# Stores into GpSimd's queue, and the loads of one batch taken apart around the transposes (Linformer attention and an MLP-mixer, one core)

## The chip, the core and the metric

The kernel runs on one core of one Trainium2 chip. The metric is the device time of one execution in microseconds; the number that counts is the median of several executions. In the text TensorE is PE, VectorE is DVE, ScalarE is ACT, GpSimd is POOL and SyncE is SP, as in the profile. "SPq" is SP's instruction queue, which only issues transfers here.

## What is computed

The inputs are q, k, v of shape (8, 8, 1024, 64): batch, heads, sequence, head size. E and F have shape (64, 1024), and there are four weight matrices. With biases and checks left out, the reference is

```python
k_proj = np.einsum('ks,bhsd->bhkd', E, k)
v_proj = np.einsum('ks,bhsd->bhkd', F, v)
scores = np.matmul(q, k_proj.transpose(0, 1, 3, 2)) / np.sqrt(64)
attn = softmax(scores)                      # over the 64 projected keys
x = np.matmul(attn, v_proj)                 # heads side by side: (8, 1024, 512)
h = np.maximum(x.transpose(0, 2, 1) @ w_tok1, 0.0) @ w_tok2   # 1024 -> 256 -> 1024
u = x + h.transpose(0, 2, 1)
h2 = np.maximum(u @ w_ch1, 0.0) @ w_ch2     # 512 -> 1536 -> 512
return (u + h2).astype(np.float32)
```

## The kernel before

The work of a batch b falls into two parts.

**The front** of a batch makes u. `kv_proj` projects k and v of all eight heads (lines 455 and 458) with copies to `kp` and `vb` by DVE and ACT; `k_transpose` (L492) turns the projected keys, and DVE and ACT copy them to `kT` (L502, L507); `scores` is one matmul per head (L555) and an exponential on ACT (L564); `attend` is four matmuls per head (L578), with a reciprocal and a multiplication on DVE (L590, L595) into `x_sb`; `token1` (L609) and `token2` (L629) are the token MLP, and DVE adds x to it (L640) into `u`. `scores` needs `qT`, which is q transposed: on PE for batches 0 and 1, and by two DMA transposes of SP (`q_transpose`, L519) for batches 2 to 7. When four of the eight row tiles of `u` are there, a DMA transpose of SP (L649) writes half of `uT`, so that each batch has a u transpose 0 and a u transpose 1, which the text calls u(b, 0) and u(b, 1).

**The back** is the channel MLP. Sub-block j = 2b + i works on half i of batch b. It begins with the sums of quarters of `uT` on DVE (`s_sums`, L671), four additions or subtractions that stand together; then `up_set` runs three sets of seven products (L801), and `down_block` seven products (L896) in the order 1, 7, 6, 2, 5, 3, 4, each product being two times six matmuls. Between products 5 and 3 of a `down_block` DVE must read a bank (`da`, L943). ACT copies other banks to `o` and `db` (L925), POOL adds u in place (L927), DVE writes the rest (L947, L955), and each sub-block stores two output tiles of 512 KB (`store`, L920). There are three output buffers, and one `db`.

Every instruction is a job of a planner (`Planner.plan`), which orders the jobs by its own estimate of times and by due times (`prio`). The jobs of PE, DVE, ACT and POOL are issued in the planned order, and each engine's queue is kept in it. Transfers are jobs on a model engine "DMA" and are put into the program where the planner's list has them; from there they stand in the queue of the engine that issues them, in order with what else this engine does. Loads of q, k and v convert from float32 to bfloat16 and are issued by POOL (L314), in pieces of four heads from batch 1 on. In the kernel before, stores and transposes are issued by SP.

`tie(j, other)` makes transfer j wait for transfer other to land. `load_batch(b)` (L979) issues all six loads of batch b after the attention of batch b - 1, tied to the transpose that was planned last (`turned[0]`); a u transpose is tied to the last load that was planned (`landed[0]`). The place where the front of a batch lies between the sub-blocks is given by due times: `front(b, at - 62, at - 14)`, where `at` is the due time of the first sub-block of batch b.

Of the kernel before, what the change touches and what calls it, by code (L numbers as in the profile page):

```python
# [34 lines left out]
class Planner:  # L35
# [4 lines left out]
    def __init__(self, caps, homes):  # L40
        self.jobs, self.caps, self.homes = [], caps, homes
        self.wrote, self.readers = {}, {}

    def add(self, eng, occ, lat, fn, reads=(), writes=(), prio=None, takes=(), uses=(), after=()):
        j = Job(len(self.jobs), eng, occ, lat, fn, prio)
# [26 lines left out]
    def plan(self):  # L72
        for j in self.jobs:
            for d in j.deps:
                d.next.append(j)
        for j in reversed(self.jobs):
            if j.prio is None:
                due = [s.prio for s in j.next]
                j.prio = (min(due) if due else 1e9) - j.occ - 0.3
        for j in self.jobs:  # L80
            if j.prio > 1e8:
                j.prio = max((d.prio for d in j.deps), default=0) + 2
        free = {}
        waiting = {j.n: len(j.deps) for j in self.jobs}
        can = {}
        est = {}

        def open_(j):
            est[j.n] = max((d.end + self.LAG[d.eng] if d.eng != j.eng else d.full for d in j.deps), default=0.0)
            can.setdefault(j.eng, []).append(j)  # L90

        for j in self.jobs:
            if not waiting[j.n]:
                open_(j)
        bank_free = [0.0] * 8
        clean = [True] * 8
        held = dict.fromkeys(self.caps, 0)
        left = {}
        for j in self.jobs:
            for b in j.banks:  # L100
                left[id(b)] = left.get(id(b), 0) + 1
        order = []
        turn = {n: [b for j in self.jobs for b in j.takes if b.stream == n] for n in self.caps}

        def home(b, now):

            if held[b.stream] == self.caps[b.stream]:
                return None
            if b.stream in "UD" and turn[b.stream][0] is not b:
                return None  # L110
            best = None
            keep = [i for i in self.homes["U"] if clean[i] and bank_free[i] is not None]
            if all(clean[:5]):
                keep = []
            for i in self.homes[b.stream]:
                t = bank_free[i]
                if t is None or (b.seeded and not clean[i]):
                    continue
                if not b.seeded and clean[i] and keep and keep[-1] == keep[0] == i:
                    continue  # L120
                c = (max(now, t), clean[i], t, i)
                if best is None or c < best:
                    best = c
            return best

        while any(can.values()):
            pick = None
            for e, js in can.items():
                f = free.get(e, 0.0)
                cands = []  # L130
                for j in js:
                    t = max(f, est[j.n])
                    spot = None
                    if j.takes:
                        h = home(j.takes[0], t)
                        if h is None:
                            continue
                        t, spot = h[0], h[3]
                    cands.append((t, j.prio, j.n, j, spot))
                if not cands:  # L140
                    continue
                t0 = min(c[0] for c in cands) + 0.02
                c = min((c for c in cands if c[0] <= t0), key=lambda c: (c[1], c[2]))
                if pick is None or c[0] < pick[0]:
                    pick = c
            if pick is None:
                raise RuntimeError("no job can go on", [(j.eng, j.fn.__qualname__, j.prio) for js in can.values() for j in js][:20], held, bank_free)
            t, _, _, j, spot = pick
            can[j.eng].remove(j)
            j.start, j.end, j.full = t, t + j.lat, t + j.lat + 0.03  # L150
            free[j.eng] = t + j.occ
            if j.takes:
                b = j.takes[0]
                b.at = spot
                turn[b.stream].remove(b)
                held[b.stream] += 1
                bank_free[spot] = None
            for b in j.banks:
                left[id(b)] -= 1
                if not left[id(b)]:  # L160
                    held[b.stream] -= 1
                    bank_free[b.at] = max(x.end for x in b.jobs) + 0.1
                    clean[b.at] = b.full
            order.append(j)
            for s in j.next:
                waiting[s.n] -= 1
                if not waiting[s.n]:
                    open_(s)
        assert len(order) == len(self.jobs), (len(order), len(self.jobs))
        return order  # L170


@with_exitstack
def kernel(
# [333 lines left out]
            writes=[("kT", 1, h) for h in heads], uses=[bk],  # L508
        )

    turned = [None]
    landed = [None]

    def q_transpose(due):
        for h in range(0, H, H // 2):
            before = turned[0]
            turned[0] = sp(
                3.5,
                lambda h=h: nc.sync.dma_start_transpose(  # L519
                    out=qT[:, h : h + H // 2].rearrange("p h j s -> p (h j) s"),  # L520
                    in_=q_sb[:, h : h + H // 2].rearrange("p h si d -> p (h si d)"),
                ),
                reads=[("q", i) for i in range(h, h + H // 2)],
                writes=[("qT", i) for i in range(h, h + H // 2)], prio=due,
            )
            if before:
                turned[0].deps.add(before)

    def q_transpose_pe(hp, due):
        bk = Bank(stream[0], full=False)  # L530
# [93 lines left out]
    def token2(b, si, due):  # L624
        bk = Bank(stream[0], full=False)

        def mm():
            for t in range(TC):
                nc.tensor.matmul(  # L629
                    bank(bk), wt2_sb[:, t, si::NSI], hT_sb[:, t, :],  # L630
                    start=(t == 0), stop=(t == TC - 1),
                )

        pe(
            TC, 512, mm, reads=["wt2"] + [("hT", t, hp) for t in range(TC) for hp in range(HP)],
            takes=[bk], prio=due,
        )
        dve(
            512,
            lambda: nc.vector.tensor_add(  # L640
                out=u_t[b % 2][:, si, :], in0=bank(bk), in1=x_sb[:, si, :]
            ),
            reads=[("x", h, si // NJ) for h in range(H)], writes=[("u", b % 2, si)], uses=[bk],
        )
        if si % NJ == NJ - 1:
            i = si // NJ
            j = sp(
                3.5,
                lambda: nc.sync.dma_start_transpose(  # L649
                    out=uT_t[i].rearrange("p s dc q -> p (s dc) q"),  # L650
                    in_=u_t[b % 2][:, i * NJ : (i + 1) * NJ].rearrange("p s d -> p (s d)"),
                ),
                reads=[("u", b % 2, n) for n in range(i * NJ, (i + 1) * NJ)],
                writes=[("uT", i, n) for n in range(HP)], prio=None,
            )
            if landed[0]:
                tie(j, landed[0])
            turned[0] = j

    def quarter(j, sh, dh):  # L660
        return uT_t[j % 2][:, 2 * sh : 2 * sh + 2, 2 * dh : 2 * dh + 2, :]
# [209 lines left out]
    def down_block(j):  # L871
# [30 lines left out]
        def product(n, i):  # L902
# [5 lines left out]
            for t in range(2):  # L908
# [5 lines left out]
                    prio=due_d(j, 2 * i + t),  # L914
                )

        def store(sh):
            rows = slice(i * NJ + 2 * sh, i * NJ + 2 * sh + 2)
            sp(
                1.5, lambda: nc.sync.dma_start(out=out_v[b, :, rows, :], in_=o_t[os[sh]]),  # L920
                reads=[o_key(sh, 0), o_key(sh, 1)], prio=None,
            )

# [52 lines left out]
            u_transpose_pe(hp, i, (-5.5 if i == 0 else 1.5) + 0.5 * hp)  # L976
    stream[0] = "F"

    def load_batch(b):  # L979
        jobs = [load_heads(b, n, hh, H // 2, None) for n in "kvq" for hh in range(0, H, H // 2)]  # L980
        for j in jobs if turned[0] else ():
            tie(j, turned[0])
        landed[0] = jobs[-1]

    def front(b, begin, end):
        units = []
# [5 lines left out]
        for i in range(H // hn):  # L992
            unit(1.9 * hn / H, lambda t, i=i: kv_proj(b, i * hn, hn, t))
            unit(0.9 * hn / H, lambda t, i=i: k_transpose(i * hn, hn, t))
            if b == 1:
                for hp in range(2 * i, 2 * i + 2):
                    unit(0.4, lambda t, hp=hp: q_transpose_pe(hp, t))
        unit(0.4, lambda t: scores(0, t))
        unit(0.4, lambda t: scores(1, t))
        for h in range(H):  # L1000
            if h + 2 < H:
                unit(0.4, lambda t, h=h: scores(h + 2, t))
            for half in range(2):
                unit(0.25, lambda t, h=h, half=half: attend(h, half, t))
        if b + 1 < B:
            unit(0.0, lambda t: load_batch(b + 1))
        for n in range(TC):
            unit(1.8, lambda t, n=n: token1(n, t))
        for si in range(NSI):
# [10 lines left out]
    for b in range(B):  # L1020
# [5 lines left out]
        if b + 1 < B:  # L1026
            at = 2 * TU * (b + 1)
            if b > 0:
                q_transpose(None)
            front(b + 1, at - 62, at - 14)  # L1030
    gate = mybir.DependencyInfo(mybir.DependencyClass.Sync, mybir.DependencyReason.DATA)
    plan = pl.plan()
# [41 lines left out]
```

The softmax here doesn't subtract the row's maximum and nothing guards it: scores larger than these inputs give would overflow.

## Time and profile before

| | |
|---|---|
| time, median of 8 runs (lowest to highest) | 440.41 us (438.84 to 440.97) |
| time of the profiled execution, and its span | 439.02 us, 437.0 us |
| mean granted clock of TensorE | 0.988 |
| busy: PE, DVE, ACT, POOL | 415.9, 320.9, 241.2, 106.3 us |
| POOL's DMA queue | 29.36 MB, 42.6% of the 16 DMA engines' span |
| SP's and ACT's DMA queue (stores, transposes) | 30.68 MB, 28.9% |
| median time to landing: store, k, v, q load | 3.6, 8.8, 12.8, 11.3 us |
| median time to landing: u transpose, q transpose | 4.6, 5.2 us |

The span is the time from the first to the last recorded instruction; about 2 us of the execution's time lie around it. Busy time of PE comes from a model of pipelined matmuls: a matmul of 256 columns is shown with 0.27 us, and in a row of them one starts every 0.109 us. The time to landing is counted from the issue and so includes time in the queue.

### The profile page before, as it was taken

What the parts mean: (1) busy time and instruction counts of PE and PEld (TensorE: products, weight loads), DVE (VectorE), ACT (ScalarE), POOL (GpSimd) and SP (SyncE); (2) the same over time, 40 slices, a digit from 0 to 9 for tenths busy, and PEclk for the clock granted to TensorE, in tenths of its full rate; (3) what the DMA queues carried; (4) which work ended last, traced back from release to release, by engine and by line L of the source; (5) the groups of instructions that cost most, each with busy time, mean ns of one, the idle gap of its engine ahead of it and who ended that gap; (6) DMA issues with size and microseconds to landing.
All of it is one profiled execution on the core that took longest, in us unless ns stands there. A gap on an engine that the chain in (4) does not pass through costs nothing.

```text
span 437.0 us, 9315 instructions
## 1 busy us (share of the span) xinstructions
PE 415.9 (95%) x3736; PEld 336.7 (77%) x3736; DVE 320.9 (73%) x783; ACT 241.2 (55%) x439; POOL 106.3 (24%) x122
## 2 busy tenths in 40 slices
PE   6689999999999999999999999999999999999993
PEld 3477878678778886788778877788768886888883
DVE  3459969679888797779697696778687596966451
ACT  1658785258545755557355654657446663555540
POOL 8542131032301332115021331115011210212212
PEclk9799999999999999999999999999999999999998
DMA  9999999198946899198955699096983711251022
GB/s 167 208 199 206 207 149 209 64 199 169 174 82 167 124 196 172 52 206 154 199 88 124 136 199 215 3 207 132 206 133 68 175 48 56 43 145 68 29 98 96
DMA packets 89515, 60.89 MB, mean 139 GB/s; under 512 B 55680, under 2 KB 84864, under 8 KB 89472
## 3 DMA queue, kind: packets, MB, share of 16 engines
q0 software_dynamic: 30624, 29.36, 42.6%
q1 hardware_dynamic: 58768, 30.68, 28.9%
q8 instruction: 29, 0.48, 0.4%
q10 hardware_dynamic: 80, 0.26, 0.3%
q14 instruction: 14, 0.11, 0.1%
HBM read 59.24 MB, written 16.78 MB: 174 GB/s over the span
## 4 chain that ended last, share of the span: by engine, by line
PE 86%; DVE 8%; ACT 3%; DMA 1%; issue 1%; DVEq 0%; ACTq 0%
PE ps L896 32%; PE ps L801 30%; PE ps L609 6%; PE ps L629 5%; PE ps L555 3%; PE ps L578 3%; PE ps L455 3%; DMA uT<-u 1%; DVE S L671 1%; DVE u L728 1%; ACT qT L547 1%; PE ps L377 1%; PE ps L539 1%; PE ps L689 1%; DVE da L943 1%
## 5 line engine op out<-in xcount | busy, mean ns | idle before, releaser
L896 PEld LDWEIGHTS <-G 128*128 128x128 bf16 x1344 | 130.1, 98 | 24.3 <-issue 5.5
L896 PE MATMUL ps<-wc_sb,G 128*128 128x256 bf16 x768 | 103.8, 273 | 3.7 <-DVE da L943 2.6
L801 PEld LDWEIGHTS <-wc_sb 128*128 128x128 bf16 x768 | 73.6, 98 | 14.3 <-issue 1.6
L823 ACT ACTIVATE G<-ps 128x512 bf16<-128x512 f32 x96 | 57.2, 599 | 39.8 <-PE ps L801 39.6
L896 PE MATMUL ps<-wT,G 128*128 128x256 bf16 x576 | 77.7, 273 | 0.0
L927 POOL TENSOR_TENSOR o<-o,u 128x512 f32<-128x512 f32 x32 | 37.6, 1175 | 129.2 <-ACT o L925 114.0
L801 PEld LDWEIGHTS <-wT 128*128 128x128 bf16 x576 | 55.1, 98 | 11.2 <-issue 2.2
L801 PE MATMUL ps<-uT,wc_sb 128*128 128x256 bf16 x384 | 57.6, 273 | 0.0
L801 PE MATMUL ps<-S,wc_sb 128*128 128x256 bf16 x384 | 57.6, 273 | 0.0
L927 POOL TENSOR_TENSOR db<-db,u 128x512 f32<-128x512 f32 x16 | 18.8, 1175 | 157.5 <-ACT db L925 157.5
L801 PE MATMUL ps<-S,wT 128*128 128x256 bf16 x384 | 54.9, 273 | 0.9 <-ACT G L823 0.7
L640 DVE TENSOR_TENSOR u<-ps,x_sb 128x512 bf16<-128x512 f32 x56 | 35.7, 684 | 22.2 <-PE ps L629 21.7
L595 DVE TENSOR_TENSOR x_sb<-ps,rdn 128x256 bf16<-128x256 f32 x128 | 49.7, 415 | 0.3
L836 DVE TENSOR_TENSOR G<-G 128x512 bf16<-128x512 bf16 x96 | 46.7, 489 | 3.4
L782 DVE CUSTOM_DVE_ANT_0 g<-ps,ub 128x512 bf16<-128x512 f32 x48 | 32.8, 684 | 20.5 <-PE ps L801 20.4
L782 DVE CUSTOM_DVE_ANT_0 G<-ps,ua 128x512 bf16<-128x512 f32 x48 | 32.8, 682 | 18.1 <-ACT ua L829 17.9
L564 ACT ACTIVATE a<-ps 128x512 bf16<-128x512 f32 x64 | 37.1, 600 | 12.2 <-PE ps L555 12.0
L829 ACT COPY ua<-ps 128x512 f32<-128x512 f32 x48 | 28.2, 587 | 24.2 <-PE ps L801 23.6
L829 ACT COPY ub<-ps 128x512 f32<-128x512 f32 x48 | 28.2, 587 | 9.6 <-PE ps L801 9.1
L842 ACT COPY ps<-ps 128x512 f32<-128x512 f32 x48 | 28.2, 588 | 6.9 <-DVE g L782 4.2
L578 PE MATMUL ps<-vb,a 128*128 128x130 bf16 x256 | 30.4, 223 | 0.6 <-DVE x_sb L595 0.6
L629 PE MATMUL ps<-hT_sb,wt_sb 128*128 128x512 bf16 x112 | 29.5, 379 | 0.0
(69 smaller groups left out, 516.0 us busy)
## 6 DMA issues: line engine op xcount, KB each, us to landing
out_dram<-o SPq DMA_DIRECT2D x32, 512.0 KB, 3.6
k_sb<-in_k_dram POOLq DMA_DIRECT2D x14, 512.0 KB, 8.8
v_sb<-in_v_dram POOLq DMA_DIRECT2D x14, 512.0 KB, 12.8
q_sb<-in_q_dram POOLq DMA_DIRECT2D x14, 512.0 KB, 11.3
wc_sb<-in_moe_w_ch_dram POOLq DMA_DIRECT2D x6, 256.0 KB, 12.6
wc_sb<-in_moe_w_ch_dram POOLq DMA_DIRECT2D x4, 384.0 KB, 12.2
k_sb<-in_k_dram POOLq DMA_DIRECT2D x4, 256.0 KB, 6.8
v_sb<-in_v_dram POOLq DMA_DIRECT2D x4, 256.0 KB, 7.3
```

The lines of the kernel that those rows point to most:

```text
L564: lambda: nc.scalar.activation(out=a_t[h % 4], in_=bank(bk), func=ACT.Exp, scale=scale),
L578: nc.tensor.matmul(view()[:, 2 * jj : 2 * jj + 2].rearrange("p c d -> p (c d)"), a_t[h % 4][:, j * P : (j + 1) * P], vb[:, h].rearrange("k ...
L595: lambda: nc.vector.tensor_tensor(out=x_sb[:, 4 * half : 4 * half + 4, h * D : (h + 1) * D], in0=view()[:, :, 0:D], in1=rdn[:, :, None].to ...
L629: nc.tensor.matmul(bank(bk), wt2_sb[:, t, si::NSI], hT_sb[:, t, :], start=(t == 0), stop=(t == TC - 1),)
L640: lambda: nc.vector.tensor_add(out=u_t[b % 2][:, si, :], in0=bank(bk), in1=x_sb[:, si, :]),
L782: nc.vector._custom_dve(TENSOR_ADD_SAT, out=out, in0=in0, in1=in1, s0=FMAX, s1=0.0)
L801: nc.tensor.matmul(t[:, c, :], w1_of(n, dd, 2 * m + c), a_of(j, n, dd), start=(n in (1, 7) and c == 0 and dd == 0), stop=(c == 1 and dd == 1),
L823: lambda: nc.scalar.activation(out=G[:, n, cs], in_=view(src), func=ACT.Relu),
L829: 512, lambda: nc.scalar.copy(out=dst, in_=view("y")), writes=[(name, s % 2)],
L836: 512, lambda: f(out=G[:, n, cs], in0=in0, in1=in1), ps=False, reads=deps,
L896: nc.tensor.matmul(view(X_OF[n])[:, t, :], G[:, G_OF[n], cc, t * P : (t + 1) * P], w2_of(n, cc), start=(n in (1, 7) and t == 0 and cc == 0 ...
L927: 512, lambda: nc.gpsimd.tensor_add(out=dst, in0=dst, in1=u_of(sh, dh)),
```

## The change

The stores of all sub-blocks but the last are issued by POOL, in the queue of the loads. `load_batch` is replaced. The k and v loads of batch b + 1 are planned right behind the projections of batch b, tied behind u(b - 1, 0); u(b - 1, 1) is tied behind the last of them. The q loads of batch b + 1 are planned behind the q transposes of batch b, which have finished with the buffer, and u(b - 1, 0) is tied behind the last of these. The planner lists a transfer by the time at which its inputs are ready, no longer by the time at which the model engine "DMA" would start it.

```diff
@@ Planner.plan
-                due = [s.prio for s in j.next]
+                due = [s.prio for s in j.next if s.prio is not None]
...
+        for g in self.groups:
+            first = min(j.prio for j in g)
+            for n, j in enumerate(g):
+                j.prio = first + 0.01 * n
...
+            j.at = est[j.n] if j.eng == "DMA" else t
...
-        return order
+        return sorted(order, key=lambda j: j.at)
@@ q_transpose
-    turned = [None]
-    landed = [None]
-
-    def q_transpose(due):
+    turned_u = {}
+
+    def q_transpose(b, behind):
         for h in range(0, H, H // 2):
-            before = turned[0]
-            turned[0] = sp(
+            j = sp(
...
-            if before:
-                turned[0].deps.add(before)
+            if behind:
+                j.deps.add(behind)
+            behind = j
+        if b + 1 < B:
+            last = load_group(b + 1, "q", j)
+            if b > 2:
+                tie(turned_u[b - 1, 0], last)
@@ token2
-            if landed[0]:
-                tie(j, landed[0])
-            turned[0] = j
+            turned_u[b, i] = j
@@ down_block
+        queue = nc.gpsimd if j < NSB - 1 else nc.sync
...
-                1.5, lambda: nc.sync.dma_start(out=out_v[b, :, rows, :], in_=o_t[os[sh]]),
+                1.5, lambda: queue.dma_start(out=out_v[b, :, rows, :], in_=o_t[os[sh]]),
@@ loads
-    def load_batch(b):
-        jobs = [load_heads(b, n, hh, H // 2, None) for n in "kvq" for hh in range(0, H, H // 2)]
-        for j in jobs if turned[0] else ():
-            tie(j, turned[0])
-        landed[0] = jobs[-1]
+    def load_group(b, names, behind):
+        jobs = [load_heads(b, n, hh, H // 2, None) for n in names for hh in range(0, H, H // 2)]
+        for j in jobs if behind else ():
+            tie(j, behind)
+        return jobs[-1]
+
+    def load_kv(b):
+        last = load_group(b, "kv", turned_u.get((b - 2, 0)))
+        if (b - 2, 1) in turned_u:
+            tie(turned_u[b - 2, 1], last)
@@ front
+        if b + 1 < B:
+            unit(0.0, lambda t: load_kv(b + 1))
+        if b == 1:
+            unit(0.0, lambda t: load_group(2, "q", None))
         unit(0.4, lambda t: scores(0, t))
...
-        if b + 1 < B:
-            unit(0.0, lambda t: load_batch(b + 1))
@@ the loop over batches
             if b > 0:
-                q_transpose(None)
+                q_transpose(b + 1, turned_u.get((b - 1, 1)))
             front(b + 1, at - 62, at - 14)
```

More of the change, by code (lines that the diff above doesn't have):

```diff
@@ L42, in __init__ @@
         self.wrote, self.readers = {}, {}
+        self.groups = []
     def add(self, eng, occ, lat, fn, reads=(), writes=(), prio=None, takes=(), uses=(), after=()):
@@ L523, in q_transpose @@
                 reads=[("q", i) for i in range(h, h + H // 2)],
-                writes=[("qT", i) for i in range(h, h + H // 2)], prio=due,
+                writes=[("qT", i) for i in range(h, h + H // 2)], prio=None,
             )
-            if before:
-                turned[0].deps.add(before)
+            if behind:
[5 more added lines that the diff above has]
+                tie(turned_u[b - 1, 0], last)
     def q_transpose_pe(hp, due):
```

## The prediction

> **What bounds the kernel now.** I read the busy times first. PE is busy in 95% of the span:
>
> ```profile
> PE 415.9 (95%) x3736; PEld 336.7 (77%) x3736; DVE 320.9 (73%) x783; ACT 241.2 (55%) x439; POOL 106.3 (24%) x122
> ```
>
> The windows of 25 us show where the rest is (the first columns are length and PE's busy time):
>
> ```profile
> 100.00:125.00 25.00, 25.00 (x209) 19.20 (x209) 22.40 (x62) 14.73 (x28) 6.81 (x8) 1.00 0.96 171
> 275.00:300.00 25.00, 24.54 (x229) 20.97 (x224) 19.38 (x40) 15.35 (x29) 5.09 (x5) 1.00 0.50 107
> 350.00:375.00 25.00, 24.45 (x201) 18.92 (x200) 20.11 (x56) 12.14 (x22) 2.31 (x2) 1.00 0.22 64
> ```
>
> PE is full from 100 to 275 us, and loses about half a microsecond in each later window. The rest is at the start (waiting for inputs) and in the last 12 us, whose order the change leaves alone. The timeline of PE names the stalls (in brackets: idle time, and who ended it):
>
> ```profile
> 91.20 0.81 PE L896 MATMUL ps<-wc_sb,G 128*128 128x256 bf16 x6 [0.85 <-DVE da L943]
> 280.61 0.82 PE L896 MATMUL ps<-wc_sb,G 128*128 128x256 bf16 x6 [0.46 <-DVE da L943]
> 325.45 0.60 PE L801 MATMUL ps<-S,wT 128*128 128x256 bf16 x4 [0.73 <-ACT G L823]
> 355.88 0.27 PE L578 MATMUL ps<-vb,a 128*128 128x130 bf16 x2 [0.55 <-DVE x_sb L595]
> 379.23 0.81 PE L896 MATMUL ps<-wc_sb,G 128*128 128x256 bf16 x6 [0.44 <-DVE da L943]
> ```
>
> Idle time starts where the modelled 0.27 us of a matmul ends, while the next could start after 0.109; so each costs 0.16 more: 3.03 + 5 x 0.16 = 3.8 us. Adding all steps (0.109 a matmul of 256 columns, 0.216 of 512, 0.057 in `attend`, 1.85 for the projections of eight heads) from matmul 790 at 88.2 us to the last gives 8.0 us less than the trace: these 3.8, 2.2 in the tail, and 2.0 in pieces of 0.25 or less. So this change, which takes no matmul away, can win 5.8 us at most.
>
> Transfers reach PE only through others. The chain of waits shows it once:
>
> ```profile
> 267.68 6.25 DMA uT<-u
> 273.95 0.43 DVE S L671
> 274.98 1.65 DVE S L671 x3
> 279.96 0.61 DVE da L943
> 280.61 0.82 PE ps L896 x6
> ```
>
> A u transpose takes 6.25 us here because loads and a store are in flight; alone it takes 4.3. DVE waits for it in its queue, and `da` and PE behind DVE.
>
> **The parts.** I compared the instruction order of both programs. PE's order is the same up to matmul 790, and the tail's. In between, scores come much earlier behind the projections: 2.0 to 2.6 us of PE work after `k_transpose` instead of 10 to 18. Token matmuls come in fours and twos between the products instead of 16 in a row. I place events of the changed program at 88.2 us plus the steps of its order.
>
> *Stores to POOL.* 30 stores leave SP. SP's waits for POOL in front of stores add up to 187.7 us, but the transposes behind them were not late for that alone: u(b, 1) must also wait for the previous odd sub-block to have read `uT1`. POOL gets 30 issues; the rows of its load issues say 0.70 to 0.87 us, so 30 x 0.77 = 23 us on an engine that is busy for 106 of 437. Behind a store POOL waits for the last DVE instruction of a sub-block; next in its queue is the `db` addition of the next sub-block, some 10 us later. An output buffer is used again 16 us or more after its store is issued, and a store lands in 2.6 to 8.8 us, or some 10 us more behind four loads. Cost: nothing; if that cover were gone, DVE's L955 would hold a bank. The Trainium skill speaks against this part: SBUF — State Buffer, "SBUF: two separate sides", says that a transfer issued by GpSimd cannot get its descriptors written while VectorE holds the shared port, and advises the queue of ScalarE or SyncE instead; it gives 3.1 us instead of 0.62 for a small transfer. By that the stores would land later, and the sum would not change, since nobody waits for them; in this trace 66 issues by POOL beside a DVE that is busy for 73% stay between 0.56 and 0.87 us.
>
> *Stalls removed.* The stall at 91.2: the new order has three scores (0.65) between product 5 and product 3 of that sub-block, so 0.65 goes. At 280.6 and 379.2 DVE came late to `da` behind the four sums S. In the new order no load is tied to run beside u(5, 0) and u(7, 0), the sums stand at 269 and 368, and the next `da` at 298 and 372: 0.62 + 0.60 go. At 325.5 ACT stood behind `kp` copies, at 355.9 DVE behind a subtraction that took 1.38 us beside a POOL addition (0.41 normally); these can come back elsewhere, so half of 0.89 + 0.72. Of the 2.0 in small pieces I take 0.5. Sum: -3.2, between -0.65 and -4.5.
>
> *Scores close behind kT.* From the last matmul of L492 to the end of ACT's copy L507 the six full-width cases took 1.99, 2.33, 2.02, 2.00, 2.59, 2.21 us. The new order leaves 1.8 us for batch 2, 2.0 for batch 3 and 2.4 for the others. Stalls with 0.1 for the semaphore: 0.3 + 0.4 + four times nothing or 0.3. I take +0.8, between 0 and 2.4 (the 2.59 for all).
>
> *The ties.* u(b, 0) waits for the two q loads of batch b + 2. Example b = 4: the q transposes follow u(3, 1) and last 9 us for two (289.02 to 297.84 in POOL's wait), so to 202; a first load lands 5.3 us after its issue (147.48 to 152.78), the next 2.55 later: 210. u(4, 0) is complete at 215. No wait; for b = 3 the q load sits behind a POOL addition and lands at 168, 2.4 us after u, but DVE has nothing to do for PE until 176. Cost: 0.
>
> u(b, 1) waits for four k and v loads, which wait for u(b, 0), for the projections of batch b + 1 and, in POOL's queue, for an addition in front. For b = 3, 4, 5 the issue comes at 175.7, 225.2 and 274.3 (projections end at 174.6, 223.9, 273.2; the addition takes 1.2). Landing of the fourth: 5.3 + 3 x 2.55 = 13.0 later, and then the transpose, 4.3 alone. But the two stores of the sub-block now sit right behind these loads in the same queue and move at the same time as the transpose, so I take the 6.25 of the row above (6.7 is the longest). Ready at 195.0, 244.5, 293.6. PE needs the sums only at 207, 256, 306, but DVE's queue has them behind reciprocals of 193.2, 242.6 and 291.9, with 0.8 of multiplications: it arrives at 194.0, 243.4, 292.7 and waits 1.0 + 1.1 + 0.9 = 3.0 us in the midst of the attention. Queued behind are reciprocals and `add_relu`, and behind those PE, which has three banks for the front and other products to run. DVE is idle for a quarter of the time and can catch up. Nothing to all of it reaches PE; I take a third, +0.9, nearest to the single case at 273.95, where 0.64 of waiting and a slow sum cost 0.62. For b = 1 (ready 110, needed by DVE at 110.9) and b = 2 (147, 150) I count 0.
>
> Sum: -3.2 + 0.8 + 0.9 = -1.5. The profiled execution took 439.02 (span 437.0 and 2 around it), so 437.5; it lies 1.39 under the median of 440.41. Taken from the median: 438.9.
>
> **Rivals.** *The stalls only move*: PE waits at kT and at the sums as much as it did at `da`. For it: both new margins are under half a microsecond. Against: the front is spread more evenly, which DVE's 22.4 us in the window from 100 to 125 shows to be needed. Price: -3.2 + 2.4 + 0.9 = +0.1, that is 440.5.
>
> *The tie blocks DVE* (slower): u(b, 1) lands later than I think, since the loads take longer. In the trace a group of loads with two stores beside it needed 16.9 us from its first issue to the fourth landing (152.87 to 169.73) where I count 13.0. With 3.9 us more, DVE waits about 4.9 us in each of three batches; at half of it on PE this is 7.4 instead of 0.9, so 440.41 + 5 = 445.4. It decides from the point where DVE waits 2.2 us in each of the three: half of 6.6 is 3.3, which with the 0.8 at kT makes up for the 3.2 and passes no change by 0.9 us. Against: with stores behind the loads and transposes kept apart, the group runs alone.
>
> *The change does not do what it says*: the tie could be dropped where two transfers share a predecessor. The order shows it in place: u(4, 1) waits for the last v load of its group.
>
> **Numbers.** The forecast has 0.55 (436.4 to 439.5), no change 0.2 (439.5 to 441.3), the blocked DVE 0.25 (441.3 to 445.4). A difference of 0.2%, 0.88 us, is about what a measurement can tell; these cases are cut there, so the chances of faster, same and slower are the same three. The range goes from 436.4, where the stalls go and almost nothing comes, to 442.8, which leaves about 0.15 out above and 0.05 below.
>
> **What would show it.** Right: no `da` stall at the first sums of a batch, no store in SP's waits, q and k/v loads in two groups per batch, DVE waiting for `uT` about 1 us near 194, 244 and 293. Wrong: DVE waiting over 2 us there, PE waiting for kT in each batch over 0.5, or POOL late with `db`.

## The result, and the profile after

The changed kernel took 443.96 us (median of 12 runs, 441.21 to 446.48), the kernel before 439.06 (33 runs, 438.78 to 442.22) in the same comparison: a ratio of 1.010, with a 95% interval of 1.0081 to 1.0119. In another comparison it was 443.37 to 440.16, or 1.0084 (1.0054 to 1.0114). The change makes the kernel slower by about 1%, 3 to 5 us, where 1.5 us less were forecast. The profiled execution took 442.56 us, with a span of 440.6.

PE's work is the same, and its busy time differs little. The busy times and the shares of the chain of waits, from the page of the kernel after:

```profile
PE 418.0 (95%) x3736; PEld 336.7 (76%) x3736; DVE 321.0 (73%) x783; ACT 242.9 (55%) x439; POOL 122.9 (28%) x152
...
PE 75%; DVE 12%; DMA 8%; ACT 2%; issue 1%; DVEq 0%; ACTq 0%
PE ps L904 26%; PE ps L809 26%; DMA uT<-u 8%; PE ps L639 5%; PE ps L619 5%; PE ps L462 3%; PE ps L588 3%; PE ps L565 3%; DVE S L679 2%; DVE x_sb L605 2%; DVE G L844 2%; DVE g L790 1%; DVE u L736 1%; PE ps L549 1%; PE ps L384 1%
```

8% of the chain that ended last, some 35 us, is now u transposes (`uT<-u`). In the kernel before all transfers together had 1%, and DVE waited for a u transpose once:

```profile
PE 86%; DVE 8%; ACT 3%; DMA 1%; issue 1%; DVEq 0%; ACTq 0%
...
DVE S L671 <- DMA uT<-u: 0.6, 1, 0.6
```

The waits of the kernel after (total, times, longest) name who stands there:

```profile
SPq L659 <- DMA v_sb<-in_v_dram: 96.7, 5, 21.6
...
DVE S L679 <- DMA uT<-u: 7.6, 6, 2.3
...
PE ps L809 <- DMA uT<-u: 2.4, 1, 2.4
...
PE ps L588 <- DVE x_sb L605: 1.7, 3, 0.9
```

The first line is the tie at work: SP holds five u(b, 1) until the last v load has landed. The second is DVE standing at the first sum of a sub-block; before, this was one wait of 0.64 us. The third is PE itself waiting for a transpose; before, this did not occur. In the fourth PE waits for the attention's multiplication, which in two of the three cases (near 251 and 302) is queued behind the sums on DVE. One such place can be read in the chain of the kernel after (start, duration, what):

```profile
244.30 6.34 DMA uT<-u
250.64 0.02 issue
250.66 0.42 DVE S L679
251.09 0.34 DVE x_sb L605
251.42 0.33 DVE S L679
...
252.07 0.43 DVE x_sb L605
252.50 0.04 issue
252.55 0.27 PE ps L588 x2
```

u(4, 1) lands at 250.64, DVE (idle, as its timeline says, for 1.55 us) has been waiting for it since 249.1, and behind the sums stand the multiplications whose banks PE needs. The timeline of PE shows the two largest stalls ahead of the tail, whose own are as before (in brackets: idle time and who ended it):

```profile
114.92 0.61 PE L809 MATMUL ps<-uT,wc_sb 128*128 128x256 bf16 x4 [2.43 <-DMA uT<-u]
...
251.48 0.27 PE L588 MATMUL ps<-vb,a 128*128 128x130 bf16 x2 [0.85 <-DVE x_sb L605]
```

The windows of 25 us at the three places shown before (length, then PE's busy time) put this in place:

```profile
100.00:125.00 25.00, 22.57 (x185) 17.55 (x183) 19.31 (x51) 12.30 (x23) 1.67 (x3) 1.00 0.99 178
275.00:300.00 25.00, 25.00 (x234) 20.41 (x232) 19.92 (x51) 17.07 (x32) 7.65 (x9) 1.00 0.81 150
350.00:375.00 25.00, 24.93 (x206) 19.81 (x204) 17.87 (x44) 11.99 (x22) 4.57 (x5) 1.00 0.20 61
```

The two later windows did become full, as forecast. The first one, which had been full, lost 2.4 us.

**A measure for what follows.** PE's order is the same in both programs up to matmul 790, and yet its start lay anywhere from 88.05 to 91.5 us in the profiled executions, with kernels of either order. In the one before and the two after, it came at 88.2, 89.2 and 91.4, and the granted clock was 0.66, 0.56 and 0.51 from 10 to 20 us, and 1.00, 0.93 and 0.64 from 20 to 30. That is not the whole reason: in the profiles of E2 and E4 below the clock was 1.00 in both stretches, and matmul 790 came at 89.7. So I compare from the start of matmul 790 to that of the last one: 342.86 us before, 345.52 after, and 347.48 in a second profile of the changed kernel (E12 below). This is the part in which PE's order differs: +2.7 and +4.6. It leaves out the first 88 us, in which the change moves some transfers but no matmul.

### The profile page after: what moved, and what is told of

Its sections match the earlier page's. It is cut to its first block, busy times and chain, and to the rows that moved or that the text cites. A ratio compares the mean times of both kernels' runs of the same rounds, so it can differ in the third digit from the quotient of the medians.

```text
span 440.6 us, 9330 instructions
## 1 busy us (share of the span) xinstructions
PE 418.0 (95%) x3736; PEld 336.7 (76%) x3736; DVE 321.0 (73%) x783; ACT 242.9 (55%) x439; POOL 122.9 (28%) x152
## 4 chain that ended last, share of the span: by engine, by line
PE 75%; DVE 12%; DMA 8%; ACT 2%; issue 1%; DVEq 0%; ACTq 0%
PE ps L904 26%; PE ps L809 26%; DMA uT<-u 8%; PE ps L639 5%; PE ps L619 5%; PE ps L462 3%; PE ps L588 3%; PE ps L565 3%; DVE S L679 2%; DVE x_sb L605 2%; DVE G L844 2%; DVE g L790 1%; DVE u L736 1%; PE ps L549 1%; PE ps L384 1%
## 5 line engine op out<-in xcount | busy, mean ns | idle before, releaser
L605 DVE TENSOR_TENSOR x_sb<-ps,rdn 128x256 bf16<-128x256 f32 x128 | 50.8, 416 | 0.7
L650 DVE TENSOR_TENSOR u<-ps,x_sb 128x512 bf16<-128x512 f32 x56 | 38.0, 687 | 10.9 <-PE ps L639 9.4
L844 DVE TENSOR_TENSOR G<-G 128x512 bf16<-128x512 bf16 x96 | 43.5, 458 | 3.3
L790 DVE CUSTOM_DVE_ANT_0 G<-ps,ua 128x512 bf16<-128x512 f32 x48 | 32.9, 685 | 13.3 <-ACT ua L837 12.7
L588 PE MATMUL ps<-vb,a 128*128 128x130 bf16 x256 | 31.8, 226 | 2.0 <-DVE x_sb L605 1.7
L639 PE MATMUL ps<-hT_sb,wt_sb 128*128 128x512 bf16 x112 | 32.5, 379 | 0.0
## 6 DMA issues: line engine op xcount, KB each, us to landing
wc_sb<-in_moe_w_ch_dram POOLq DMA_DIRECT2D x4, 384.0 KB, 12.1
```

Source lines behind the costliest of these rows:

```text
L588: nc.tensor.matmul(view()[:, 2 * jj : 2 * jj + 2].rearrange("p c d -> p (c d)"), a_t[h % 4][:, j * P : (j + 1) * P], vb[:, h].rearrange("k ...
L605: lambda: nc.vector.tensor_tensor(out=x_sb[:, 4 * half : 4 * half + 4, h * D : (h + 1) * D], in0=view()[:, :, 0:D], in1=rdn[:, :, None].to ...
L639: nc.tensor.matmul(bank(bk), wt2_sb[:, t, si::NSI], hT_sb[:, t, :], start=(t == 0), stop=(t == TC - 1),)
L650: lambda: nc.vector.tensor_add(out=u_t[b % 2][:, si, :], in0=bank(bk), in1=x_sb[:, si, :]),
L790: nc.vector._custom_dve(TENSOR_ADD_SAT, out=out, in0=in0, in1=in1, s0=FMAX, s1=0.0)
L844: 512, lambda: f(out=G[:, n, cs], in0=in0, in1=in1), ps=False, reads=deps,
```

## The experiments

All runs were compared with the kernel before on the same chip; E1 to E8 ran on one chip, E9 to E12 on another. Theory A: the ties make u(b, 1) late. Theory B: the stores, in a queue of their own beside the transposes, make u(b, 1) late. Theory C: the new order of PE's work costs the time, whatever the transfers do. After eight runs three more were stated: P (what costs time is how late the transposes are against the place that the planner gave the sums), and its rivals Q (later sums are better in any arrangement) and R (the new order that a longer estimate brings makes the difference, whatever the waits).

**E1: no u transpose waits for loads.** The order of all engines stays that of the kernel after.

```diff
-        if j in tied and tied[j] is not shown:
+        if j in tied and tied[j] is not shown and j not in turned_u.values():
```

> The changed kernel in its own planned order, but no u transpose waits for loads any more (the ties stay in the planner; only the waits are left out). Theory A, the ties make u(b, 1) late and PE and DVE wait for it: the 2.4 us of PE at sub-block 3 and most of the 7.6 us that DVE waits for uT go, and the time falls by 3 to 5 us, to that of the kernel before or below it. Theory B, stores in a queue of their own slow the transposes beside them: the transposes still take 5 to 7 us, and the time falls by less than 1.5 us. Theory C, the new interleaving of PE and DVE is what costs: less than 1 us.

440.2 us, ratio 1.0004 (0.9978 to 1.003): 3.8 us less than the changed kernel. The stall at 115 is gone, since u(1, 1) lands at 95.1. But DVE still waits, and the rows of the `uT` tile in this kernel say why:

```profile
  DVE S L679: 7.8, 5
...
DMA to landing us min/median/max: 4.2/7.1/13.3
```

Without the tie u(2, 1) to u(5, 1) are issued 8 to 13 us earlier, at 134.6, 184.6, 235.2 and 286.9, and take 11.2, 12.4, 13.3 and 12.1 us, while loads and stores run at the same time. The last three land at 197.0, 248.5 and 299.0 where the changed kernel has 200.0, 250.6 and 300.5, and matmul 790 and the missing stall at 115 already explain 3.8 us of that. From matmul 790 on this kernel takes 344.47 us, 1.0 less than the first profile of the changed kernel and 3.0 less than the second. So the tie is not the only cause: it trades a late start for a short transfer.

**E2: stores stay on SP, ties kept.**

```diff
-        queue = nc.gpsimd if j < NSB - 1 else nc.sync
+        queue = nc.sync
```

> The changed kernel with all stores back on SP; loads, ties and planned order of PE, DVE and ACT as changed. Theory A: the ties are still there, so the waits for uT stay: within 1 us of the changed kernel. Theory B: transposes after the loads take 4.3 to 5 us instead of 5 to 7, the fourth load of a group lands 1 us earlier, and the time falls by 2 to 4 us. Theory C: within 1 us.

455.44 us, ratio 1.0328 (1.0276 to 1.0379), the slowest of all. Four of the five tied transposes of odd sub-blocks take 4.4 us, but all are released late: the stores now run beside the loads, and the fourth load of a group lands 17.3 to 18.4 us after the first issue, where the changed kernel has 14.0 to 15.4. What the profile says of DVE and PE in this kernel:

```profile
DVE S L679 <- DMA uT<-u: 14.5, 6, 4.5
...
PE ps L809 <- DMA uT<-u: 4.6, 1, 4.6
```

None of the theories had expected this (within 1 us by A and C, 2 to 4 us faster by B). Under these ties the change needs its other half: the stores behind the loads in one queue are worth 11.5 us (in the profiles, 10.9 from matmul 790 on, which takes 356.37 here).

**E3: the kernel before, with its stores (but the last two) on POOL and nothing else changed.**

```diff
-                1.5, lambda: nc.sync.dma_start(out=out_v[b, :, rows, :], in_=o_t[os[sh]]),
+                1.5, lambda: (nc.gpsimd if j < NSB - 1 else nc.sync).dma_start(
+                    out=out_v[b, :, rows, :], in_=o_t[os[sh]]),
```

> The kernel before with its stores, but for the last two, on POOL and nothing else changed. Theory B: transposes get longer beside stores, and the time rises by 1 to 3 us over the kernel before. Theories A and C: there is no tie and no new order here, so it stays within 0.5 us of the kernel before.

449.74 us, ratio 1.0242 (1.0198 to 1.0285). Here no tie is new. In the kernel before a store stands in SP's queue, so a transpose behind it cannot start ahead of it; here u(b, 1) runs beside two stores. The rows of its `uT` tile:

```profile
  DVE S L671: 12.3, 6
...
DMA to landing us min/median/max: 4.3/5.8/11.1
```

So "stores to POOL", which the prediction put at nothing, costs 10 us when it is done alone, where B had 1 to 3. In its profile 6.8 of them lie behind matmul 790 (349.65); the rest is a later matmul 790 (91.5), of which the part that the stores have is not known.

**E4: only u(1, 1) is free of its tie.**

```diff
+        if j in tied and tied[j] is not shown and j is not turned_u[1, 1]:
```

> The changed kernel without one wait: u(1, 1) no longer waits for the k and v loads of batch 3. Theory A: the 2.4 us of PE at sub-block 3 go and nothing else, so the time falls by 2 to 3 us and stays above that without any of the waits. Theories B and C: within 1 us of the changed kernel.

441.1 us, ratio 1.0027 (1.0006 to 1.0048): of the 3.8 us of E1, 2.9 come with this one tie. That agrees with the stall of 2.4 us in the profile; the intervals of E1 and E4 overlap, so what the other ties cost is not separated from nothing. Its own profile is of a long execution (445.22), and I read nothing from it.

**E5 and E6: the planner is told that u(b, 1) end 4 us later**, so that it puts the sums of odd sub-blocks, and the products that use them, later. E5 also frees u(1, 1) of its tie; E6 keeps all ties.

```diff
             turned_u[b, i] = j
+            if i == 1:
+                j.lat += 4.0
```

> The changed kernel with u(1, 1) free of its tie, and with the planner told that the transposes u(b, 1) end 4 us later than it assumed, so that it puts the sums S of odd sub-blocks later in DVE's order (on the scale of the steps at 113, 150, 199 to 207, 247.6, 295.4, 340 and 383.5 us). Theory A and B together (what is left over the kernel before, after the tie on u(1, 1), is DVE that stands at the sums waiting for late transposes, whatever makes them late): DVE's waits for uT fall to under 0.5 us each, and the time to 438 to 439.5, at or under the kernel before. Theory C (the new interleaving itself, scores close behind kT and matmuls of the token phase in small pieces, costs the rest): 441, as with the tie on u(1, 1) taken away alone.

> The same late sums, with the tie on u(1, 1) kept. Theory A and B: the stall of 2.4 us of PE at 114.9 stays or grows to the part that the later place does not cover, so 2 to 3 us more than with late sums and without that tie, about 441. Theory C: 443 to 444, as the changed kernel. If it equals the kernel with late sums and without the tie, the tie on u(1, 1) costs only because DVE's order was planned too early.

437.75 (ratio 0.995, 0.9933 to 0.9967) and 437.67 (0.9944, 0.9928 to 0.9961). Both are faster than the kernel before, and they are equal. E6 has every transfer, queue and tie of the changed kernel; its u(1, 1) still lands at 114.2. Yet from matmul 790 on it takes 340.53 us instead of 345.52. Its waits:

```profile
DVE S L681 <- DMA uT<-u: 2.2, 2, 1.8
```

and none of PE for `uT`. That speaks against theory C, but does not settle it, since PE's order is not the same: at 724 of the 2946 places from matmul 790 on another kind of matmul stands than in the changed kernel. E8 settles it. My expectation for E6 was wrong by 3 us: I had held the stall at 115 to be a price of the tie, but with other products in front of those of u(1, 1) PE does not get there before 115.

**E7: E5 with the stores of sub-blocks 10 to 14 back on SP**, in one queue with the transposes.

```diff
-        queue = nc.gpsimd if j < NSB - 1 else nc.sync
+        queue = nc.gpsimd if j < 10 else nc.sync
```

> Late sums and no tie on u(1, 1), and the stores of sub-blocks 10 to 15 go back to SP, where they stand in one queue with the transposes, after the loads of batch 7 have ended. Theory B (a store in a queue of its own beside a transpose lengthens it): u(6, 1) and u(7, 1) take 4.3 to 5 us instead of 7.1 to 7.3, and the time is 0 to 1 us under the kernel with late sums alone. If transposes there stay at 7 us, the store's queue is not what lengthens them.

438.22 us, ratio 0.997 (0.9942 to 0.9998): the same as E5 within the intervals, so the gain did not come. The transposes did: u(6, 1) took 5.0 us and u(7, 1) 4.3, where E5 has 7.3 and 6.8 with no loads around. So here the store in another queue is what lengthens them; with the sums planned late it no longer matters.

**E8: the changed kernel without its stores**, but for those of the last sub-block. The stores are left out, and with them most of the output; ties and the order of PE, DVE and ACT stay: in the two traces PE's matmuls from 790 on and DVE's instructions have the same order throughout.

> The changed kernel with its ties, and all stores but those of the last sub-block left out, so most of the output is not written; the order of PE, DVE and ACT is the same. Theory A (the ties alone make the transposes late): the fourth load of k and v still lands 13 us after the first issue, u(1, 1) lands 0 to 2 us earlier than in the changed kernel, DVE's waits at the odd sums stay at 0.5 us or more in most batches, and the time is 442 to 444. Theory B (the stores beside loads and transposes make them late): u(b, 1) take 4.3 to 4.6 us, DVE's waits for uT vanish but at u(1, 1), where under 1 us is left, and the time is 439 to 440.5.

438.56 us, ratio 0.9974 (0.9956 to 0.9992). The rows of the `uT` tile in this kernel, where the kernel after has 7.6 us of waiting and 4.2/5.4/7.3:

```profile
  DVE S L679: 1.3, 1
...
DMA to landing us min/median/max: 4.2/4.4/6.1
```

Theory B holds for most of the transposes and of the waits. Two of the seven u(b, 1) lie outside the 4.3 to 4.6 us that it gave: u(3, 1) with 5.4, and u(4, 1) with 6.1, which has neither a load nor a store beside it. The wait of 1.3 us that is left is behind this one, with 1.1 us of PE, so the stores don't explain most of the 1.3 us near 251 in the changed kernel. B doesn't hold for the loads: the five groups took 15.3, 13.4, 14.3, 14.1 and 14.5 us from the first issue to the fourth landing, much as with the stores behind them in the queue (15.4, 14.2, 14.8, 14.1, 14.0). u(1, 1) landed at 110.6 instead of 114.9: 1.1 of that is the earlier matmul 790, 1.7 an earlier start of its loads (u(1, 0) took 4.45 instead of 5.34, and POOL issued the first load 0.6 after it instead of 1.4), and 1.4 its own transfer. From matmul 790 on: 341.56 us, 1.3 less than the kernel before. So theory C falls: with the changed kernel's order, but without the stores, nothing is lost.

**E9, E10, E11: how late, and in which kernel.** E9 is the kernel before with the same 4 us, E10 the changed kernel with 2, E11 with 6 (all ties kept). E12 is the changed kernel again.

> The kernel before with the planner told that u(b, 1) end 4 us later. Theory P (the sums stood too early only because the change made u(b, 1) late; later sums are no gain in themselves): the kernel before had one wait of 0.64 us for uT, and that on an even sub-block, so its time stays within 0.5 us of 440 or gets worse. Rival Q (later sums are better in any arrangement, and the 6 us between the changed kernel and the one with late sums have nothing to do with the transfers): the kernel before gains 2 us or more as well, to 438 or less.

> The changed kernel with u(b, 1) planned 2 us later instead of 4, ties kept. Sums of odd sub-blocks stand in the plan at 111.3, 149.6, 196.5, 244.1, 293.4, 339.2 and 383.5 us. Theory P (price per microsecond of lateness of the transposes over the plan): DVE still waits for about a third of the 7.6 us (u(1, 1) lands some 3 us after the plan), and the time lies between the two kernels, at 439.5 to 441. Rival R (the new order of PE that the longer estimate brings makes the difference, whatever the waits): it has no value for 2 us but one of the ends, 437.7 or 444, and does not follow the waits.

> The changed kernel with u(b, 1) planned 6 us later, ties kept. Theory P: with 4 us two waits of 2.2 us in all are left; with 6 none over 0.3, which wins 0 to 0.5 us over 4, while the products come closer to the end of their sub-block, so 437 to 438.5. Rival R: a time that does not follow the waits, 439 or more.

> The changed kernel itself, a second time, for a second profile and for a comparison on the same chip with the two above. Theory P: 443 to 445; a profiled execution that is longer than the first shows it in waits for uT, since nothing else in the first profile depends on how fast the transfers run.

| | time, us | ratio to before (95%) | DVE waits for uT, us (times) |
|---|---|---|---|
| E9, before, +4 | 438.15 | 0.9958 (0.994 to 0.9977) | 0 |
| E10, after, +2 | 437.28 | 0.995 (0.9923 to 0.9977) | 1.1 (1) |
| E11, after, +6 | 437.51 | 0.9942 (0.9925 to 0.9959) | 0.2 (1) |
| E12, after | 443.37 | 1.0084 (1.0054 to 1.0114) | 8.6 (7) |

The four expectations stand above in the order of this table. The waits of E12:

```profile
DVE S L679 <- DMA uT<-u: 8.6, 7, 3.0
...
PE ps L809 <- DMA uT<-u: 3.7, 2, 3.1
```

Its part from matmul 790 on is 2.0 us longer than in the first profile. Waits of DVE and PE for `uT` add up to 12.3 instead of 10.0, and u(1, 0) took 8.5 us instead of 5.3 beside the q loads. This kernel's time depends on how its transfers meet.

For P and R: 2, 4 and 6 us give the same time (340.48, 340.53 and 340.38 us from matmul 790 on). E10 does not lie between, as I expected of P: with 2 us most waits were gone already (DVE's 1.1 us and 1.0 of PE at 114.3 are left), where I had thought that a third of DVE's would stay. The time follows the waits, and not the amount of delay; but since all three sit at one end, they don't refute R by themselves. E8 does: it has the changed kernel's order and, but for u(4, 1), no late transposes, and is within 1.2 us of that end.

For Q: the kernel before gains 2.0 us too (1.85 by the ratio; 1.2 from matmul 790 on, 341.66), though it had just one wait of 0.6 for `uT`. I had allowed 0.5 for P. Its profile no longer shows the stalls of ACT's `G` and of `x_sb`, and the `da` stall at 280.6 is down to 0.27; there are new ones of 0.48 at 134.9 and 0.66 at 330.9. So a part of the gain from later sums is a luckier order that has nothing to do with late transfers, and with the sums planned later the time of the changed kernel (0.995) can't be told apart from that of the old one (0.9958).

## Why the prediction was wrong

**The steps that failed are the ties, put at +0.9 us, and the stores to POOL, put at nothing.** In the first profile the direct stalls are 2.6 us behind u(1, 1) and, behind DVE's late sums, 1.3 near 251, 1.0 near 302 and 0.5 at 395: together 5.4, idle time plus the 0.16 of each. With the 0.9 of two new stalls at 141.07 and 149.96, which other work of DVE makes, and without the 3.8 of the stalls that the prediction names, that is +2.5, near the +2.7 measured. E8 tells how much of it comes with the stores: 345.52 - 341.56 = 4.0, and 5.9 against the second profile. The parts of the step:

- *"For b = 1 I count 0"* was the largest error, 2.6 us. The text had u(1, 1) ready at 110, and DVE there at 110.9. It came at 114.9, of which 1.0 is the later matmul 790. The group's first issue was at 93.60, since u(1, 0) had taken 5.34 us beside the q loads; the fourth load landed 15.4 later, not 13.0; the transpose took 5.8. A margin of 0.9 us does not bear three such terms, and this one lay directly in front of PE's products.
- *The landing of four loads, 13.0 us*: it was 14.0 to 15.4, and E8 shows that the stores behind them have no part in that. The term was too small by itself: 5.5 us or more to the first landing and 2.5 to 4.0 for each that follows, in place of 5.3 and 2.55.
- *DVE's wait of 1.0 + 1.1 + 0.9 near 194, 244 and 293*: none, 1.55 and 0.54, and 2.34 at 115, 0.79 at 347 and 2.01 at 393. The last two are batches 6 and 7, for which nothing was counted: no load and no tie is there, but two stores in POOL's queue beside the transpose, which takes 7.3 and 7.1 us instead of 4.3 and 4.3. That is the stores' part, put at "nothing"; "nobody waits for them", it said. Nobody waits for the stores; but the transposes wait beside them.
- *A third of DVE's wait reaches PE*: of the 4.1 us of waiting near 251, 300 and 393, 2.8 did. The order that the prediction itself described, with the attention's reciprocals and multiplications right behind the sums, was reason to take more. The row at 273.95, 0.62 of 0.64, was nearer than the third.
- *The 6.25 us of a transpose*: the prediction gives loads and a store in flight as the reason. The size was near for u(1, 1) and u(4, 1), but the 6.1 us of u(4, 1) in E8 show that such a time comes without either.

**What was right.** The stalls named in the profile before are gone from those places, and no store stands in SP's waits but the last ones. POOL's issues did not get longer: 96 of them took 0.53 to 0.87 us each. Scores close behind kT cost 0.14 us, at 91.35, not 0.8 (the upper bound of this term, 2.4, should be 2.7 by its own numbers). Without the lateness the sum would have been -3.2 + 0.8 = -2.4; E8, whose order is that of the changed kernel, is at -1.3 from matmul 790 on, with 1.3 us of waiting left, and E6, E10 and E11 at -2.3 to -2.5, though part of that is the luck that E9 shows. So the removal was about the right size, as far as this luck lets one see, and the cover was misjudged.

**The rival** "the tie blocks DVE" had the right sign and came near in time (445.4), but not by its own point of decision: in its three batches DVE waited 0, 1.55 and 0.54 us, and the groups of loads took 14.0 to 14.8 us there, not 16.9. Of the 5.4 us, 2.3 stand in batches that it names; 2.6 came from one place that it did not name, and 0.5 from a batch without a tie.

**Open.** How much of the 6 us between the changed kernel and E10 is lateness, and how much is order, is only bounded: E8 leaves at most 1.2 us of it to order against the first profile. Why u(4, 1) takes 6.1 us in E8 without loads and stores, no run shows; the last section says what moves beside it. Why the first 88 us vary, I did not try to find out.

## What to carry to other kernels

When a wait is moved onto a transfer, compute the landing with everything that the change puts beside it in other queues, and set that against the time at which the in-order engine reaches its consumer; a margin below a microsecond is none. A planner that orders an engine's queue must be told the transfer time under load: two microseconds more in one estimate were worth 6 us here, and taking away every tie only 4. But try the same in the kernel before: there 4 us more brought 2. One half of a two-part change alone (E2, E3) can be far worse than either kernel.

## What the runs showed of the hardware

A transposing transfer can take three times as long beside others. The same u transpose took 4.2 to 4.5 us in nine of fourteen cases of E8, the kernel without stores, 5.0 right behind a store in its own queue (E7, one case), 6.8 to 7.3 beside two stores of another queue, and 11.2 to 13.3 beside four loads and two stores (E1). The other five of E8, with no load beside them either, took 4.9 to 6.1, u(3, 0) and u(4, 1) the longest. What sets these five apart from the nine is a packet of 8 or 16 KB in the queues that the pages call `instruction` (q8 and q14), which moves while they do. In all fourteen profiles together, 40 u transposes had no load, store or such packet beside them, and took 4.2 to 4.5 us; 43 had such a packet, but no load or store, and 39 of these took longer than every one of the 40. No run takes that packet away, so the cause is not shown. A plain store, too, took 2.6 to 8.8 us in the kernel before, so it is not shown that a transpose suffers more than others. The page of the kernel after gives a reason to suspect, which no run here isolates (queue, packets, MB, share):

```profile
q0 software_dynamic: 34944, 45.09, 51.0%
q1 hardware_dynamic: 54448, 14.95, 20.1%
```

The second queue, which carries the transposes, moves a quarter of the bytes with three fifths of the packets, 275 bytes in a packet against 1290. The Trainium skill (DMA: Bandwidth & Descriptors, "Queues, rings and completion order") states that a DMA engine takes turns between the queues that have work for it, a packet of each at a time. Whether its packets are those that the profile counts is not shown. If they are, that would let a queue of small packets fall behind one of large packets, which goes with the 7.3 us beside two stores of the other queue against 5.0 behind a store of its own; the row can't show the turns themselves. What the trace does show: the packets of u(6, 1) are busy for as long beside the stores as alone (38.0% of the 16 engines in 7.35 us in the kernel after, 66.0% in 4.24 us in E8, 2.8 us each), so the longer time lies between its packets. Also not expected: stores behind the loads in one queue cost the loads nothing that can be seen (E8), though they are issued while the loads still move; the same stores in another queue delay the fourth load by 2 to 4 us (E2).
